# LayerNorm of the GLU's first tile placed among the last forward segments; weight turns, last turns and stores regrouped around it

## The chip, the cores and the metric

The kernel runs on one core of a Trainium2 chip. The metric is the device time of one execution in microseconds (us), taken as the median over runs. A core has a matrix engine (TensorE, "PE" in the profile, with its weight loads listed as "PEld"), a vector engine (VectorE, "DVE"), a scalar engine (ScalarE, "ACT"), a general engine (GpSimd, "POOL") and a synchronisation engine (SyncE, "SP"). Each runs its own instructions in program order; semaphores order them against each other. SP and POOL issue nearly all DMA transfers of this kernel, each on its own queue.

## The reference, cut to what matters

The computation is one block with adaptive normalisation, forward and backward. Inputs are bfloat16, x is 2048 rows of 512.

```python
mod = (silu(c) @ w_mod).reshape(1, 6, 1, -1)
sa, ca, ga, sb, cb, gb = mod[:, 0], ..., mod[:, 5]
h = layernorm(x) * (1 + ca) + sa
x = x + ga * A(h, mem0, Wq, Wk, Wv, Wo)       # attention in 64 segments
h = layernorm(x) * (1 + cb) + sb
x = x + gb * B(h, w_gate, w_up, w_down)       # GLU, F = 1792
```

A works through 64 segments of 32 rows. Each segment puts 8 memory rows ahead of its 32, projects to q, k and v (32 heads of 128), applies a masked softmax, and projects back; the first 8 rows of the result are the memory of the next segment, so the segments form a chain. B is `(sigmoid(g) * u) @ w_down` with `g = h @ w_gate` and `u = h @ w_up`. The outputs are x and the gradients of x, mem0, the seven weight matrices, c and w_mod, twelve in all, for a given `grad_out`.

## The kernel before, in words

The program has stages one after the other: the first norm and the six modulation vectors (phase 1, worked in pieces inside phase 2), the forward attention (phase 2, L437 to 962), the GLU forward and backward (phase 3, L990 on), then its weight gradients and the backward attention.

**The end of phase 2.** The loop over the 64 segments `s` (NS = 64, `s4 = s % 4`) writes, for each, in this order: k and q projections (`proj`), v projection (`v_chunk`), scores and exponentials (`st_exp`), sums of the softmax (`den`), products with v (`pv`, copies `ost`), the turned attention output (`ott`), the output projection (`outproj`, `evac_turned`), the split of its result into a high and a low bfloat16 part which TensorE adds again (`split_pair`, `sum_pair`: the tiles `at_hi`, `at_tb`, `ao_b_hi`, `ao_b_lo`), and stores for the backward pass: `OSR`, `OT` and the attention rows `AOA` in the segment, `VT` and `PS` (turned v and turned, normalised probabilities) by the function `norm` (L942), which the next segment runs. The tiles `VTr` and `Pst` are turned by a transposing DMA in all segments but the last; of segment 63 they are turned by TensorE after the loop (L951 to 961), `Pst` with the product on DVE, `VTr` with copies on ScalarE. `tail` is work put off from earlier segments (gathered rows whose projection TensorE does in chunks), and `tail.finish` ends it. `self.pin(i0)` keeps each engine's instructions in the order in which they are written.

Segment 63 also prepares phase 3. The GLU's weights and buffers lie in memory of the attention weights that have been read for the last time (`glu_tiles`, L964): w_down, the four broadcast vectors `bcs[2..5]` (ga, sb, 1 + cb, gb, each 128 x 512 in f32) and the input rings in Wv, w_gate and w_up in Wk, w_gateT and w_upT in Wq. POOL's queue loads w_gate (L834), w_up (L883) and w_down (L884); SP's queue loads the broadcasts (`mod_bc`, L369) and the rows of tile 0 and, after the loop, tile 1 (`glu_load`, L984 to 987: x, four pieces of AOA, grad_out). Both queues hold eight transfers: the profile shows an issue waiting for the transfer eight before it.

**Phase 3.** The 2048 rows form 16 tiles of 128 (NT). `run_pipeline` runs seven stages s0 to s6, one iteration after the other, in each iteration the deepest first: in iteration `it` stage `sK` works on tile `it - K`. Those that matter here:

- s0 (L1053 to 1085) is LayerNorm of a tile: DVE forms x1 = x + ga * a and its statistics, POOL the reciprocal root by a power, DVE `xhf`, the modulated rows `h2` and the gated gradient `db = gb * grad_out`; ScalarE copies `xh2`; POOL stores h2 and db (H2ROWS, DBROWS).
- s1 (L1089 and L1090) turns h2 and db into `hdT` by two transposing DMAs on SP.
- s2 (L1111 and L1115) multiplies hdT with w_gate and w_up; ScalarE applies the sigmoid (L1112).
- s3 (L1138) multiplies the turned db with w_downT; s4 (L1153) and s5 (L1178) go on with the results, with w_gateT and w_upT.

The three turned weights are made by TensorE through two buffers of PSUM (`psT`, tile `tp`), each filled by eight 128 x 128 turns at most and then copied out. w_gate's 56 turns (`wT_piece`, L1027) all stand before the pipeline, with copies on ScalarE; the dictionary `turns` (L1043) puts w_down's 56 (`wdT_piece`, L1038) at the end of iteration 2, behind s2 of tile 0, with copies alternating between DVE and ScalarE, and w_up's in iterations 3 (32) and 4 (24), alternating too.

## Time and profile before

| what | value |
|---|---|
| runs | 3063.09, 3070.22 and 3066.83 us, median 3066.83 |
| the profiled execution | 3072.34 us, its span 3070.5 us, mean granted clock 0.99 |
| busy share of TensorE, DVE, ScalarE, POOL | 97%, 52%, 42%, 40% |
| TensorE busy, 940 to 960 us | 17.90 of 20 |
| DMA share of the span's 16 engines, queue 1 and queue 0 | 62.5% and 15.5% |

The page covers one execution. Times in a list of instructions run from the span's start. A line of the timeline gives the start, the duration, the engine, the source line, the operation, output and inputs, the shape, the count, and in square brackets the time for which the engine was idle before and what released it. "tp<-ident,Wk" is a turn of w_gate or w_up, "tp<-ident,Wv" one of w_down, since the GLU's tiles are named after the memory that they lie in; for the same reason "Wq" as an output is w_gateT, w_upT or, behind the change, tile 0's rows. "PEclk" is the clock that TensorE was granted, as a share of full speed. Up to 980 us the trace shows the forward segments, from 980 on the GLU.

### The profile page before, as it was taken

What the parts mean: (1) busy time and instruction counts of PE and PEld (TensorE: products, weight loads), DVE (VectorE), ACT (ScalarE), POOL (GpSimd) and SP (SyncE); (2) the same over time, 40 slices, a digit from 0 to 9 for tenths busy, and PEclk for the clock granted to TensorE, in tenths of its full rate; (3) what the DMA queues carried; (4) which work ended last, traced back from release to release, by engine and by line L of the source; (5) the groups of instructions that cost most, each with busy time, mean ns of one, the idle gap of its engine ahead of it and who ended that gap; (6) DMA issues with size and microseconds to landing.
All of it is one profiled execution on the core that took longest, in us unless ns stands there. A gap on an engine that the chain in (4) does not pass through costs nothing.

```text
span 3070.5 us, 106490 instructions
## 1 busy us (share of the span) xinstructions
PE 2970.5 (97%) x44213; PEld 1860.3 (61%) x44289; DVE 1607.4 (52%) x3746; ACT 1286.6 (42%) x3179; POOL 1213.9 (40%) x2640
## 2 busy tenths in 40 slices
PE   5999999999997999989899999999999999999999
PEld 3666666666665444445577777777777754445454
DVE  5656656656655888732255555555555632322221
ACT  2555555555554444322255555555555520111011
POOL 2555554555554222211344444444444422333321
PEclk8999999999999999989999999999999999999999
DMA  9877877877788899987599999999999998666574
GB/s 300 217 221 204 220 216 208 220 212 209 214 219 247 200 229 232 226 264 240 169 247 245 245 251 240 249 247 247 248 242 252 244 281 268 208 193 220 185 238 148
DMA packets 839319, 703.53 MB, mean 229 GB/s; under 512 B 539730, under 2 KB 711794, under 8 KB 837940
## 3 DMA queue, kind: packets, MB, share of 16 engines
q1 hardware_dynamic: 713668, 486.69, 62.5%
q0 software_dynamic: 54512, 148.63, 15.5%
q10 hardware_dynamic: 70656, 61.41, 6.4%
q8 instruction: 348, 5.70, 0.8%
q14 instruction: 135, 1.11, 0.1%
HBM read 294.93 MB, written 276.35 MB: 186 GB/s over the span
## 4 chain that ended last, share of the span: by engine, by line
PE 47%; issue 2%; DMA 1%; POOL 0%; SPq 0%; ACT 0%; DVE 0%; POOLq 0%
PE gps L1987 11%; PE dh_ps L215 8%; PE g_ps L1649 6%; PE pass_ps L255 5%; PE gps5o L2001 4%; PE dhq_ps L223 4%; PE dh_tps L215 3%; PE dp_ps L1626 2%; PE tps L1559 2%; PE dp_ps L1634 1%; PE turn_ps L1513 1%; PE dh_ft L323 1%; POOL out_dram L1991 0%; DMA rows<-OSR 0%; DMA rows_x<-dQT 0%
## 5 line engine op out<-in xcount | busy, mean ns | idle before, releaser
L1987 PE MATMUL gps<-rows,hrows 128*128 128x512 bf16 (+2 forms) x2124 | 415.6, 355 | 1.9
L1987 PEld LDWEIGHTS <-hrows 128*128 128x128 bf16 x2160 | 211.2, 98 | 204.6
L63 DVE CAST ot<-gps 128x512 bf16<-128x512 f32 (+3 forms) x76 | 48.1, 633 | 297.1 <-PE gps L1987 200.4
L1693 POOL COPY dOst<-RAd 96x512 bf16<-96x512 bf16 x128 | 75.2, 612 | 308.9 <-DVE RAd L63 308.9
L61 ACT ACTIVATE ot<-gps 128x512 bf16<-128x512 f32 (+3 forms) x75 | 41.3, 551 | 356.4 <-PE gps L1987 241.8
L656 PE MATMUL pass_ps<-Wv,hT 128*32 128x512 bf16 (+2 forms) x2304 | 188.2, 357 | 0.0
L1991 POOL DMA_DIRECT2D out_dram<-ot x108 | 81.4, 754 | 261.4 <-DVE ot L63 135.6
L255 PEld LDWEIGHTS <-hT 128*32 128x32 bf16 x4096 | 125.0, 97 | 95.8 <-DMA Wq<-in_A_Wq_dram 6.3
L942 POOL TENSOR_TENSOR Pst<-Pst,rden 120x1408 bf16<-120x1408 bf16 x63 | 159.9, 2538 | 35.2 <-issue 22.0
L61 ACT ACTIVATE dVT<-g_ps 128x480 bf16<-128x480 f32 (+1 forms) x192 | 104.6, 545 | 96.6 <-PE g_ps L1649 96.1
L63 DVE CAST Vst<-pass_ps 96x512 bf16<-96x512 f32 x128 | 87.3, 682 | 107.5 <-ACT RBv L61 103.2
L215 PE MATMUL dh_ps<-WvT,dVT 128*32 128x512 bf16 x2048 | 134.2, 382 | 0.1
L255 PE MATMUL pass_ps<-Wq,hT 128*32 128x512 bf16 x2048 | 125.6, 383 | 6.1 <-DMA Wq<-in_A_Wq_dram 6.1
L2001 PE MATMUL gps5o<-WoT,rows 128*128 128x512 bf16 x580 | 127.8, 379 | 3.4 <-DMA rows<-OSR 2.8
L223 PE MATMUL at_ps<-Wo,OT 128*32 128x256 bf16 x4096 | 125.4, 275 | 5.2 <-DMA Wo<-in_A_Wo_dram 4.9
L656 PE MATMUL pass_ps<-Wv,hb 128*32 128x512 bf16 (+2 forms) x636 | 127.2, 345 | 0.0
L255 PE MATMUL pass_ps<-Wk,hT 128*32 128x512 bf16 x2048 | 124.1, 379 | 1.8 <-POOL hT L545 1.1
L731 POOL DMA_DIRECT2D Vst<-RBv x192 | 99.5, 523 | 62.1 <-ACT ET L778 39.2
L255 PE MATMUL pass_ps<-WoT,dyT 128*32 128x256 bf16 (+1 forms) x3072 | 122.4, 308 | 0.9 <-ACT dyT L1767 0.9
L223 PE MATMUL dhq_ps<-WqT,dQT 128*32 128x256 bf16 x4096 | 122.9, 273 | 0.0
L215 PE MATMUL dh_ps<-WkT,dKT 128*32 128x512 bf16 x2048 | 122.3, 380 | 0.0
L223 PEld LDWEIGHTS <-dQT 128*32 128x32 bf16 x4096 | 109.6, 97 | 15.9
(413 smaller groups left out, 6991.5 us busy)
## 6 DMA issues: line engine op xcount, KB each, us to landing
OSR<-Ost SPq DMA_DIRECT2D x64, 352.0 KB
OT<-OT SPq DMA_DIRECT2D x64, 352.0 KB
VT<-VTr SPq DMA_DIRECT2D x64, 352.0 KB
PS<-Pst SPq DMA_DIRECT2D x64, 352.0 KB
OT_l<-OT SPq DMA_DIRECT2D x64, 352.0 KB
Pst_l<-PS SPq DMA_DIRECT2D x64, 352.0 KB
VT_l<-VT SPq DMA_DIRECT2D x64, 352.0 KB
DVR<-rows_x POOLq DMA_DIRECT2D x64, 352.0 KB, 6.1
```

The costliest lines, as they stand in the source:

```text
L61: return nc.scalar.activation(out, in_, AF.Copy)
L63: return nc.vector.tensor_copy(out, in_)
L215: self.nc.tensor.matmul(ps[32 * j:32 * j + 32, :], lhsT=lhsT, rhs=w, start=(n < 4), stop=(n >= total - 4), tile_position=(0, 32 * j))
L223: nc.tensor.matmul(ps[32 * j:32 * j + 32, :], lhsT=x[k], rhs=w[k][:, 256 * d:256 * d + 256], start=(n == 0), stop=(n == total - 1), tile_p ...
L255: self.nc.tensor.matmul(ps[32 * j:32 * j + 32, :], lhsT=lhs(c), rhs=rhs, start=(c == 0), stop=(c == DC - 1), tile_position=(0, 32 * j))
L656: nc.tensor.matmul(ps[32 * j:32 * j + 32, o * E:(o + n) * E], lhsT=lhsT, rhs=wc[:, 3 * a + hl:3 * (a + n - 1) + hl + 1:3, :], start=(c == ...
L731: nc.gpsimd.dma_start(Vst[96 + 8 * j:104 + 8 * j, :], rb[32 * j + o:32 * j + o + 8, :])
L942: nc.gpsimd.tensor_tensor(Pst[0:120, :, :], Pst[0:120, :, :], rden[:, :].unsqueeze(2).to_broadcast([120, G, 128]), op=ALU.mult)
L1649: nc.tensor.matmul(ps[:, j, 0:w], lhsT=lh[:, g * GW:(g + 1) * GW], rhs=rh[:, g * GW:g * GW + w], start=True, stop=True)
L1987: nc.tensor.matmul(ps[:, 0:ng * E], lhsT=hrows[:, tp_, c * 128:(c + 1) * 128], rhs=rows[:, tp_, 0:ng * E], start=(tp_ == 0), stop=(tp_ == ...
L1991: nc.gpsimd.dma_start(outw[c * 128:(c + 1) * 128, h0:h0 + 3 * (ng - 1) + 1:3, :], ot[:, 0:ng * E].rearrange("p (h e) -> p h e", e=E))
L2001: nc.tensor.matmul(pss[gg][:], lhsT=src[0][:, src[1], gg * E:(gg + 1) * E], rhs=dyrows[:, tp_, :], start=(tp_ == order[0]), stop=(tp_ == o ...
```

## The change

LayerNorm of tile 0 leaves the pipeline (`s0` and `s1` return at once for j = 0) and becomes nine steps that stand in the last four segments. In segment 60 SP loads x, AOA and grad_out of tile 0, in 61 the four broadcasts, in 62 DVE forms the two gated products; in 63 follow the add (before `proj`), the statistics and the power (before `v_chunk`), the scaling, then the modulated rows and ScalarE's copy (after `outproj`), POOL's copies of the broadcasts into `bcs`, and eight turns of h2 and db on TensorE with one copy by ScalarE into `first_hdT`, in place of the two transposing DMAs. The buffers are those of phase 2 that are no longer in use, and two new small tiles in Wq's pool. A sigmoid of one column is added on ScalarE in segment 63.

The turns of segment 63 move: those of v into the segment, with copies on DVE in place of ScalarE, the store VT ahead of OSR's; those of the probabilities partly into the segment, partly ahead of `tail.finish`, with the store PS. The load of w_down moves behind `ott`; the rows of tile 1 are loaded in the segment, and what is left of tile 0's loads after it (`glu_load(0)` without x) behind PS's store.

w_gate's turns move from ahead of the pipeline into the iterations: 16 in 2 (behind w_down's), 40 in 3; w_up's are now 16 in 3 and 40 in 4. All of these are copied by ScalarE.

```diff
--- before.py
+++ after.py
...
         Wq = self.Wq = wq.tile([128, DC, H * E], BF16, name="Wq")
+        self.first_x1 = wq.tile([128, D], F32, name="x1_0")
+        self.first_st = wq.tile([128, 12], F32, name="st_0")
...
+            def first_tile_steps():
+                f32 = lambda t: t.bitcast(F32)
+                x0, ar, h2 = RB["k"][:, 0:D], RB["k"][:, D:2 * D], RB["k"][:, 0:D]
+                dout, db = RB["q"][:, 0:D], RB["q"][:, D:2 * D]
+                xhf = f32(RBv[NT % 2][:, 0:2 * D])
+                bc = {2: self.sa_bc[:], 4: self.ca1_bc[:]}
+                x1, sm = self.first_x1, self.first_st
+                def load():
+                    nc.sync.dma_start(x0, io["A_x"].rearrange("o s d -> (o s) d")[0:128, :])
+                    for i in range(4):
+                        nc.sync.dma_start(ar[32 * i:32 * i + 32, :], self.AOA[i + 1, M:M + T, :])
+                    nc.sync.dma_start(dout, io["grad_out"].rearrange("o s d -> (o s) d")[0:128, :])
+                    nc.gpsimd.memset(sm[:, 10:11], -0.5)
+                def load_mod():
+                    for i, x in ((3, "k"), (5, "q")):
+                        bc[i] = f32(btails[NT - 2][x][:].rearrange("p i x -> p (i x)"))
+                    for i in (2, 5, 4, 3):
+                        nc.sync.dma_start(bc[i], self.MODROW[:, i * D:(i + 1) * D].rearrange("o d -> (o d)").partition_broadcast(128))
+                def gates():
+                    nc.vector.tensor_tensor(db, dout, bc[5], op=ALU.mult)
+                    nc.gpsimd.dma_start(self.DBROWS[0:128, :], db)
+                    nc.vector.tensor_tensor(x1[:], ar, bc[2], op=ALU.mult)
+                def add():
+                    nc.vector.tensor_tensor(x1[:], x1[:], x0, op=ALU.add)
+                def stats():
+                    nc.vector.bn_stats(sm[:, 0:6], x1[:])
+                    nc.vector.bn_aggr(sm[:, 6:8], sm[:, 0:6])
+                    nc.vector.tensor_scalar_add(sm[:, 8:9], sm[:, 7:8], EPS)
+                    nc.gpsimd.tensor_tensor(sm[:, 9:10], sm[:, 8:9], sm[:, 10:11], op=ALU.pow)
+                def scale():
+                    nc.vector.tensor_scalar(xhf, x1[:], sm[:, 6:7], sm[:, 9:10], op0=ALU.subtract, op1=ALU.mult)
+                def rows():
+                    nc.scalar.activation(self.first_xh2, xhf, AF.Copy)
+                    nc.vector.scalar_tensor_tensor(out=xhf, in0=bc[4], scalar=1.0, in1=xhf, op0=ALU.add, op1=ALU.mult)
+                    nc.vector.tensor_tensor(h2, xhf, bc[3], op=ALU.add)
+                    nc.gpsimd.dma_start(self.H2ROWS[0:128, :], h2)
+                def mods():
+                    for i in (2, 5, 3):
+                        nc.gpsimd.tensor_copy(self.bcs[i], bc[i])
+                    nc.gpsimd.tensor_scalar_add(self.bcs[4], bc[4], 1.0)
+                def turn():
+                    tp = psp.tile([128, 2 * DC, 128], BF16, name="hd_tp", tag="p")
+                    for i in range(2 * DC):
+                        src = h2 if i < DC else db
+                        nc.tensor.transpose(tp[:, i, :], src[:, (i % DC) * 128:(i % DC) * 128 + 128], self.ident[:, :])
+                    nc.scalar.activation(self.first_hdT, tp[:], AF.Copy)
+                return load, load_mod, gates, add, stats, scale, rows, mods, turn
+            first_tile = first_tile_steps()
...
+                def turn_v(pi):
+                    ps, n = transposes_part(Vst, pi)
+                    self.evac("dve", VTr[:, pi * PG:pi * PG + n, :], ps)
+                def turn_p(pi):
+                    ps, n = transposes_part(ET, pi)
+                    nc.vector.tensor_copy(Pst[96:128, pi * PG:pi * PG + n, :], ps[96:128])
+                    nc.vector.tensor_tensor(Pst[0:120, pi * PG:pi * PG + n, :], ps[0:120],
+                                            rden[:, pi * PG:pi * PG + n].unsqueeze(2).to_broadcast([120, n, 128]), op=ALU.mult)
                 def ost(pi, or_ps, eng):
                     n = min(PG, G - pi * PG)
                     if eng == "act":
...
                 if s < NS - 1 and norms:
                     norms.pop()()
+                if s == NS - 1:
+                    first_tile[3]()
                 proj("k", 0, "dve")
                 proj("k", 1, "act")
                 if s == NS - 1:
...
                         p1(1, k)
                     v_first()
                     v_tails(0)
+                if s == NS - 1:
+                    first_tile[4]()
                 v_chunk(s, 0)
                 turns()
                 v_chunk(s, 1)
                 if s == NS - 1:
                     v_chunk(s, 2)
+                    first_tile[5]()
                 if s == 0:
                     p1(P1_AHEAD, 0)
                 if s == NS - 1:
-                    for i in (2, 4, 3, 5):
-                        self.mod_bc(None, i, "", t=self.bcs[i])
-                    self.glu_first = {0: self.glu_load(0, nc.sync)}
                     late_rows()
+                    self.glu_first = {1: self.glu_load(1, nc.sync)}
                 st_exp(0)
                 st_exp(1)
                 st_exp(2)
+                if s == NS - 1:
+                    turn_v(0)
+                    turn_v(1)
                 if s + 1 < NS:
                     v_chunk(s, 2)
                     v_tails(s + 1)
...
                     nc.sync.dma_start(Pst[:], ET[:, :], transpose=True)
                 else:
                     nc.gpsimd.dma_start(self.w_up, io["B_w_up"].rearrange("(c p) f -> p c f", p=128))
-                    nc.gpsimd.dma_start(self.w_down, io["B_w_down"].rearrange("(fc p) d -> p fc d", p=128))
                 or1 = pv(1)
                 ost(0, or0, "dve")
                 ost(1, or1, "act")
...
                 recip(2, 3, or2)
                 ost(2, or2, "dve")
                 fill(s4, "turn")
+                if s == NS - 1:
+                    turn_v(2)
                 ott(0)
                 if more:
                     mask_mm(more.pop(0))
...
                 if not early:
                     self.pop_later()
                 self.pop_later()
+                if s == NS - 1:
+                    nc.gpsimd.dma_start(self.w_down, io["B_w_down"].rearrange("(fc p) d -> p fc d", p=128))
+                    nc.sync.dma_start(self.VT[s], VTr[:])
                 nc.sync.dma_start(self.OSR[s], gl3(Ost))
                 at_ps = outproj()
                 evac_turned()
                 if s4 < 3:
                     p1(s // nseg_t + P1_AHEAD, s4 + 1)
+                if NS - 4 <= s < NS - 1:
+                    first_tile[s - NS + 4]()
+                elif s == NS - 1:
+                    first_tile[6]()
                 if s + 1 < NS:
                     tails_in("kq", s + 1)
                 parts = self.split_pair(sb2, at_ps, "at")
                 tail.collect(s4, [OT])
                 nc.sync.dma_start(self.OT[s], gl3(OT))
                 fill(s4, "f1")
+                if s == NS - 1:
+                    first_tile[7]()
+                    nc.scalar.activation(self.first_st[:, 11:12], self.first_st[:, 10:11], AF.Sigmoid)
                 if s4 == 3:
                     tail.chunk()
+                if s == NS - 1:
+                    turn_p(0)
+                    first_tile[8]()
                 ft = self.sum_pair(psp, parts, "at", "p")
                 if hT_next is not None:
                     nc.scalar.activation(hT_next[:, :, 0:M], ft[:, :, 0:M], AF.Copy)
...
                 if s < NS - 1:
                     norms.append(norm)
-            self.glu_first[1] = self.glu_load(1, nc.sync)
+            turn_p(1)
+            turn_p(2)
+            nc.sync.dma_start(self.PS[NS - 1], Pst[:])
+            self.glu_first[0] = self.glu_load(0, nc.sync)
             tail.finish()
-            for pi in range(NP):
-                ps, n = transposes_part(ET, pi)
-                nc.vector.tensor_copy(Pst[96:128, pi * PG:pi * PG + n, :], ps[96:128])
-                nc.vector.tensor_tensor(Pst[0:120, pi * PG:pi * PG + n, :], ps[0:120],
-                                        rden[:, pi * PG:pi * PG + n].unsqueeze(2).to_broadcast([120, n, 128]), op=ALU.mult)
-            nc.sync.dma_start(self.PS[NS - 1], Pst[:])
-            for pi in range(NP):
-                ps, n = transposes_part(Vst, pi)
-                self.evac("act", VTr[:, pi * PG:pi * PG + n, :], ps)
-            nc.sync.dma_start(self.VT[NS - 1], VTr[:])
-            nc.vector.tensor_scalar_add(self.bcs[4], self.bcs[4], 1.0)
             self.pinned = self.pin(i0)
     def glu_tiles(self):
...
         self.w_gateT = self.flat(Wq, 0, n).rearrange("p (c d) -> p c d", c=FC)
         self.w_upT = self.flat(Wq, n, n).rearrange("p (c d) -> p c d", c=FC)
         self.ring_dout += [self.flat(Wq, 2 * n, D)]
+        self.first_hdT = self.flat(Wq, 2 * n + D, 2 * D).rearrange("p (c x) -> p c x", x=128)
+        self.first_xh2 = self.flat(Wq, 2 * n + 3 * D, D)
     def glu_load(self, j, q):
-        q.dma_start(x0, io["A_x"].rearrange("o s d -> (o s) d")[r0:r1, :])
+        if j > 0:
+            q.dma_start(x0, io["A_x"].rearrange("o s d -> (o s) d")[r0:r1, :])
         for i in range(4):
             q.dma_start(a_rows[32 * i:32 * i + 32, :], self.AOA[4 * j + i + 1, self.cfg.M:self.cfg.M + self.cfg.T, :])
         q.dma_start(dout, io["grad_out"].rearrange("o s d -> (o s) d")[r0:r1, :])
...
-            turns = {2: [wdT_piece(c) for c in range(DC)],
-                     3: [wT_piece(w_up, w_upT, 0, 8, 0)], 4: [wT_piece(w_up, w_upT, 8, 6, 0)]}
+            turns = {2: [wdT_piece(c) for c in range(DC)] + [wT_piece(w_gate, w_gateT, 0, 4, None)],
+                     3: [wT_piece(w_gate, w_gateT, 4, 10, None), wT_piece(w_up, w_upT, 0, 4, None)],
+                     4: [wT_piece(w_up, w_upT, 4, 10, None)]}
...
                 load(j + 1)
                 st = ins.pop(j)
+                if j == 0:
+                    st.update(x1=self.first_x1, rstd=self.first_st[:, 9:10], xh2=self.first_xh2)
+                    return st
                 a_rows = st["a_rows"]
...
                 return st
             def s1(j, st):
+                if j == 0:
+                    st["hdT"] = self.first_hdT
+                    return st
                 hdT = sbp.tile([128, 2 * DC, 128], BF16, name="hdT", bufs=2)
                 nc.sync.dma_start(hdT[:, 0:DC, :], st["h2"][:], transpose=True)
                 nc.sync.dma_start(hdT[:, DC:2 * DC, :], st["db"][:], transpose=True)
...
             ET = mybir.EngineType
-            wT_piece(w_gate, w_gateT, 0, FC, None)()
             later = after
             def after(it):
```

## The prediction

> **What bounds the kernel now.** I read the page first: TensorE is busy for 2970.5 of 3070.5 us, 97%, and the costliest lines of the chain of waits are all TensorE's, so time is won only where TensorE stands still. The 40 slices show one dip at slice 13. The table of stages, cut into 20 us pieces, puts it between the last forward segment and the GLU (columns: stretch, length, busy us of PE, PEld, DVE, ACT, POOL, then granted clock, DMA share, GB/s).
>
> ```profile
> 960.00:980.00 20.00, 17.53 (x314) 11.46 (x307) 9.94 (x27) 8.48 (x23) 8.38 (x11) 0.97 0.98 354
> 980.00:1000.00 20.00, 5.36 (x60) 4.34 (x59) 12.10 (x24) 9.98 (x13) 5.03 (x11) 0.67 0.70 218
> ...
> 1020.00:1040.00 20.00, 17.76 (x128) 10.16 (x128) 16.80 (x28) 9.90 (x16) 5.52 (x10) 1.00 1.00 238
> 1040.00:1060.00 20.00, 19.95 (x104) 9.57 (x104) 16.28 (x31) 7.48 (x13) 3.81 (x7) 1.00 0.90 211
> ```
>
> From 1040 on TensorE is full, so whatever the stretch 960 to 1044 gains stays gained to the end. The timeline there, in order of time, names the waits:
>
> ```profile
> 976.17 0.69 DVE L313 TENSOR_TENSOR ao_b_lo<-ao_tps,ao_b_hi 128x512 bf16<-128x512 f32 x1 [0.87 <-ACT ao_b_hi L312]
> ...
> 978.59 0.43 DVE L953 COPY Pst<-tps 32x512 bf16<-32x512 bf16 x1
> 979.05 0.69 DVE L954 TENSOR_TENSOR Pst<-tps,rden 120x512 bf16<-120x512 bf16 x1
> ...
> 980.09 1.91 PE L1027 MATMUL tp<-ident,Wk 128*128 128x128 bf16 x16
> ...
> 983.84 1.47 POOL L709 DMA_DIRECT2D AOA<-ao_b_rb  x3 [3.01 <-DMA Wv<-in_B_w_down_dram]
> ...
> 985.61 0.69 DVE L1059 TENSOR_TENSOR t<-Wv 128x512 f32<-128x512 bf16 x1 [3.36 <-DMA Wv<-AOA]
> ...
> 997.23 1.20 SPq L1089 DMA_TRANSPOSE hdT<-h  x1
> ...
> 999.68 1.67 PE L1111 MATMUL mm<-Wk,hdT 128*128 128x448 bf16 x4 [13.15 <-DMA hdT<-h]
> ...
> 1007.14 0.94 PE L1038 MATMUL tp<-ident,Wv 128*128 128x128 bf16 x14
> ...
> 1007.73 0.62 DVE L63 COPY w_downT<-tp 128x896 bf16<-128x896 bf16 x1 [2.04 <-PE tp L1038]
> ...
> 1014.30 0.92 PE L1111 MATMUL mm<-Wk,hdT 128*128 128x448 bf16 x4
> ...
> 1022.06 1.00 ACT L61 ACTIVATE Wq<-tp 128x1024 bf16<-128x1024 bf16 x1
> ...
> 1029.17 0.92 PE L1111 MATMUL mm<-Wk,hdT 128*128 128x448 bf16 x4
> ...
> 1044.26 3.19 PE L1153 MATMUL mm<-Wv,hhT 128*128 128x512 bf16 x14
> ```
>
> TensorE turns w_gate (980.09 to 986.5) and then stands for 13.15 us until the transposed rows of tile 0 arrive; stage s2 of tile 0 starts at 999.68. That is the prize. The reader should also see two smaller things: POOL waited 3.01 us for w_down to land, at 983.84, and DVE had all of LayerNorm of tiles 0, 1 and 2 behind it before the first w_downT copy at 1007.73.
>
> **The change, part by part.** Times below are the profiled execution's (span 3070.5 us, 3072.34 us in all; the median of the runs shown, 3066.83, is 5.5 lower). Its marks are carried forward from the order in which the built instructions stand on each engine.
>
> *Early loads and the first norm (segments 60 to 63).* SP gets six more issues (x rows, four of AOA, grad_out; some 0.45 us each by L984, L986, L987) ahead of OT's store in segment 60, and the four broadcasts (2.03 us by L369) in 61. OT's next write is 10 us after its store, so 3 us are covered; without that slack ScalarE and DVE would wait for the store up to that length. The broadcasts leave the stretch 965 to 983, where SP's next issues waited 3.4, 3.3, 2.2 and 2.0 us for them. DVE's seven added operations fall into its idle times: two products (0.69 each) into 2.13 us before at_lo, the add into 0.76, statistics (0.69, 0.18, 0.15) into 1.03, the scaling (0.55) and two VTr copies (0.43 each) into 1.83. POOL's power (0.57) makes w_up's issue 0.7 late, the DBROWS issue (0.54) delays only tail copies that nothing needs for 7 us. Cost nothing, up to 0.5 us if a cover fails.
>
> *The tail of segment 63.* The third VTr copy (0.36) stands before OT's copy: the output projection slips 0.36. ScalarE gets the xh2 copy (0.63) in an idle 1.19, then table load 1.28, a Sigmoid of one column (0.20, as L156's) and the hdT copy (1.02 by the 128x1024 copies) before ao_b_hi: at_hi ends 972.30, table and Sigmoid 973.8, hdT 974.87, ao_b_hi 975.5 instead of 974.24. DVE then does ao_b_lo, at_tb and the turns of P 1 and 2 (2.06 us, 979.77 to 981.83 before) ahead of the last ao_b_lo, which slips from 976.17 to 978.6 (the first Pst copy, at 973.4, needs segment 62's PS store, which SP's wait shows landed at 970.3). The chain behind it is 1.94 us to TensorE's end (978.11) and 2.37 to DVE's: TensorE is free for the GLU at about 980.6, DVE at 981.0.
>
> The page "ScalarE: Activation LUTs" (Trainium skill, section "What ACT_TABLE_LOAD costs") adds a drain of 1.38 us to the 1.28 of a table load; the trace's load at 47.61 is followed by its ACTIVATE at 48.90, with no drain. By the page DVE would be free 1.4 later, at 982.4, and POOL's wait, below, would still end later: the sum would be the same.
>
> *POOL.* The four copies of the broadcasts to Wv have no row (f32 to f32): between four of the 0.76 cast and four of the 1.55 product, 3.0 to 6.2 us from 973.4; I take 3.0 (the cast is the nearer form). Both ends lie before its next work at 980.2, so either costs nothing. w_down's issue (1.10) moves from 965.38 to 970.8. POOL then issues nine AOA stores (0.5 each); the seventh needs w_down landed, as it did before (the 3.01 us), and behind them stands the power of tile 1. When does w_down land? Before, it took 18.4 us from issue to 983.84 among as many bytes: 1.0 MB of broadcasts and 0.4 of tile 0 go from this stretch, 1.1 MB of VT, OSR and OT stores and most of a PS store come in. It queues behind w_up either way, so I take 984.5; ends 982 (w_up out of the way sooner) and 989.2 (18.4 us from the new issue). Two more stores, a memset and the semaphore put the power's start 1.7 later, 986.2, and xhf of tile 1 at 986.85; without w_down it would be 985.65.
>
> *DVE in the GLU.* s0 of tile 0 is gone, but s0 of tiles 1 and 2 now start at 981 instead of 994 and 999.86, and all of it stands before the first w_downT copy. From xhf of tile 1 to the end of tile 2's db the rows show 997.34 to 1005.69, 8.35 us: the first w_downT copy starts at 995.2 (before 1007.73), 10.7 after w_down. s2 of tile 0 runs at 980.6; TensorE was nearly idle from 977, so I charge the half clock (0.50 in the stretch after the old wait) for its first 3.7 us: end 988.5. It turns 14 blocks of w_down and then waits for DVE and ScalarE, some 5 us: s2's early start is not the path, DVE is. So the new waits of s2's first Sigmoid and u for the stores of VT and OSR, whose memory they reuse, have 5 us of cover.
>
> *To s2 of tile 1.* Before, 6.57 us from that copy to 1014.30. Added: 16 turns of w_gate (0.9) and a new half-clock start, some 0.2: 995.2 + 7.7 = 1002.9. Gain 11.4 here.
>
> *The turns of w_gate and w_up, now 56 and 40 in iterations 3 and 4 (32 and 24 before), all copied by ScalarE.* In 3, s2 of tile 1 ends at 1008.95, but ScalarE first has xh2 of tile 3, whose xhf DVE ends 9.2 after the last w_downT copy (1000.0, as before): the last u ends at 1011.0. Seven copies at 1.02 and 0.01 between follow; TensorE's last turns need the fifth (1016.15), then come four matmuls of s4 and, at 1017.5, s3 (3.02): s2 of tile 2 at 1020.5 against 1029.17. The gain falls to 8.7. In 4, xhf of tile 4 ends 10.6 after s3's start (1026.15 to 1036.79 before), at 1028.1; xh2 and u, then five copies, the fifth to 1034.5; two matmuls and 14 of dgT: s4 of tile 1 at 1038.0 against 1044.26. Before, DVE took half of these copies, 0.64 each.
>
> **Sum: 6.3 us.** In parts: s2's start 19.1 earlier; less 6.6 for the wait behind DVE's two norms (12.5 left), 1.1 for the new turns and clock (11.4), 2.7 for seven copies in iteration 3 (8.7), 2.4 for five in 4 (6.3). Profiled execution 3072.3 to 3066.0; median 3066.8 to 3060.5.
>
> TensorE then has one new wait of 2.35 us in iteration 4 (1028.1 to 1030.45). Rows bound its clock: a wait of 1.48 at 1037.4 left it at 1.00, the thin stretch from 975.5 brought it to 0.50 for 3.3 us. I take no drop, the nearer row, and keep 1.6 us for the range. The page "TensorE: Matmul & The Clock Gate" (Trainium skill, section "What's actually happening") lowers the clock after an idle window of about 3.4 us, which gives none here and a drop in the 5 us wait ahead of w_downT; the sum by it is the same 6.3.
>
> **Rivals.** (1) *The copies and POOL cost less*: w_down is early (gain 1.2), the 128x1024 copies run at the 0.93 mean of 981.19 to 987.7 (12 times 0.09, 1.1), and the P turns don't delay the tail (2.0): 4.3 more, 3056.2. For it: that mean; against: the copies in the GLU took 1.00 to 1.02. (2) *w_down as late as its new issue*: 989.2, every microsecond costs one: 6.3 less 4.7, 3065.2. For it: the POOL wait; against: w_up was in front in both. (3) *Slower: SP's queue*. Behind PS's store (978.8) stand ten issues up to tile 2's AOA rows, each waiting for the one eight before it to land. At the 0.55 of 985 to 997 with PS's wait they land at 987.5, and DVE needs them at 989.35. At the 2.5 of 970 to 983 (970.29, 973.88, 977.65, 980.04, 982.59) they land at 1006: 16.6 late, 3077. It breaks even at 995.6, 1.5 us an issue. Against: w_gate and w_up are then gone. (4) *The change wins all its 19 us*: not possible while the w_downT copies stand behind two norms on DVE; under 2%.
>
> **Chances and range.** About 0.2%, 6.1 us, is what a measurement of this kernel tells from none. Main case 0.50, half of it beyond 6.1; rival 1 0.22, rival 2 0.18, rival 3 0.10. So faster 0.47, same 0.43, slower 0.10. The range runs from rival 1 less 1.7 us of the runs' own spread (3054.5) to a break-even plus 2 (3069); rival 3 beyond that is left out.
>
> **What would show it.** Right: the first s2 matmul at 979 to 983 with no wait on hdT; the first w_downT copy of DVE at 994 to 998, at the end of an unbroken s0 of tile 2, with a TensorE wait of 4 to 6 us before it; a POOL wait on w_down before the last AOA stores; seven Wq copies in a row on ScalarE and TensorE waiting for them. Wrong: w_downT copied before 992, or a DVE wait on AOA rows ahead of tile 2's t, or a lower clock after 1025.

## The result, and the profile after

The changed kernel takes 3061.01 us in the median of 22 runs (3055.93 to 3064.80), the kernel before 3066.36 in as many. The ratio is 0.9979 with a 95% interval of 0.9973 to 0.9985, a gain of 0.21% where 0.2% was forecast (3060.5 us).

Single executions of one kernel spread by 9 to 11 us, more than the gain, so the traces are compared from a common point: the first k projection of segment 58, at 887.24 us of the span before and 883.76 after. (The texts of e9 and e11 call it that of segment 60. Counted back from segment 63, the last one, segment 60's own comes 28.86 us later in both traces; the change begins behind that.) The last point taken is the first modulation sum of s6 (the matmuls into `acc_ps`, 1056.45 before and 1047.40 after), from where TensorE is full. From there to the end the fourteen profiles of this study take 2006.9 to 2015.6 us. Before and e2, which run the same code there, take 2014.1 and 2007.3, so I read that part as jitter. Between the two points lie 169.21 us before and 163.64 after: the change is worth 5.57 us in its own stretch.

The stages of the changed kernel (columns as in the table before):

```profile
960.00:980.00 20.00, 17.11 (x280) 10.81 (x278) 12.99 (x34) 9.65 (x23) 10.61 (x18) 1.00 1.02 381
980.00:1000.00 20.00, 13.40 (x110) 8.03 (x109) 16.04 (x28) 10.35 (x16) 5.40 (x11) 0.91 0.65 194
1000.00:1020.00 20.00, 18.02 (x124) 10.64 (x123) 11.64 (x19) 12.52 (x18) 3.75 (x7) 0.91 0.94 202
1020.00:1040.00 20.00, 17.94 (x117) 9.55 (x116) 12.55 (x24) 10.78 (x16) 3.38 (x7) 1.00 0.63 158
1040.00:1060.00 20.00, 20.00 (x106) 9.68 (x105) 17.65 (x33) 7.47 (x13) 5.45 (x10) 1.00 0.91 219
```

TensorE is busy for 13.40 of the 20 us from 980 on, where it had 5.36, but it is not full again before 1040: three stretches hold 10.6 us of gaps together. Its timeline names most of them:

```profile
976.89 0.92 PE L1205 MATMUL mm<-Wk,Wq 128*128 128x448 bf16 x4
...
985.05 1.55 PE L1209 MATMUL mm<-Wk,Wq 128*128 128x448 bf16 x4 [4.21 <-ACT sg L1206]
986.39 1.70 PE L1205 MATMUL mm<-Wk,Wq 128*128 128x448 bf16 x4
...
991.67 0.55 PE L1125 MATMUL tp<-ident,Wv 128*128 128x128 bf16 x7 [1.73 <-ACT w_downT L61]
...
999.23 0.92 PE L1205 MATMUL mm<-Wk,hdT 128*128 128x448 bf16 x4
...
1008.30 0.82 PE L1247 MATMUL mm<-Wv,hhT 128*128 128x512 bf16 x3 [1.96 <-DMA hhT<-hh]
...
1018.43 0.92 PE L1205 MATMUL mm<-Wk,hdT 128*128 128x448 bf16 x4
...
1028.10 0.61 PE L1114 MATMUL tp<-ident,Wk 128*128 128x128 bf16 x8 [1.92 <-ACT Wq L61]
```

The 13.15 us for hdT are gone: s2 of tile 0 starts as soon as the tail of the segments ends. In their place stand 4.21 us in the middle of s2, 1.73 for the copies of w_downT, 1.96 for the transposed hh and 1.92 for the copies of w_upT. On DVE, ScalarE and POOL:

```profile
980.04 0.69 DVE L1150 TENSOR_TENSOR t<-Wv 128x512 f32<-128x512 bf16 x1 [2.72 <-DMA Wv<-AOA]
...
986.37 0.69 DVE L1150 TENSOR_TENSOR t<-Wv 128x512 f32<-128x512 bf16 x1 [0.42 <-DMA Wv<-AOA]
...
991.52 0.68 DVE L1173 TENSOR_TENSOR db<-Wk,Wv 128x512 bf16<-128x512 bf16 x1
992.12 1.15 DVE L63 COPY w_downT<-tp 128x896 bf16<-128x896 bf16 x2
```

```profile
968.69 1.28 ACT L1008 ACT_TABLE_LOAD   x1
969.98 0.20 ACT L1008 ACTIVATE st<-st 128x1 f32<-128x1 f32 x1
...
983.93 0.63 ACT L1166 ACTIVATE xh<-xhf 128x512 bf16<-128x512 f32 x1 [9.70 <-DVE xhf L1165]
984.47 0.53 ACT L1206 ACTIVATE sg<-mm 128x448 bf16<-128x448 f32 x1
...
1027.03 4.67 ACT L61 ACTIVATE Wq<-tp 128x1024 bf16<-128x1024 bf16 x5
```

```profile
979.86 0.99 POOL L771 DMA_DIRECT2D AOA<-ao_b_rb  x2 [0.27 <-DMA Wv<-in_B_w_down_dram]
...
982.05 0.50 POOL L771 DMA_DIRECT2D AOA<-ao_b_rb  x1 [1.20 <-DMA AOA<-at_rb]
...
982.74 0.58 POOL L1161 TENSOR_TENSOR rstd<-ve,mhalf 128x1 f32<-128x1 f32 x1
```

DVE's first copy of w_downT follows the last product of tile 2's norm with no gap, and ScalarE's first sigmoid follows the copy xh2 of tile 1, for which it had stood 9.70 us.

### The profile page after: what moved, and what is told of

It is laid out like the page before. It is cut to its first block, busy times and chain, and to the rows that moved or that the text cites. A ratio compares the mean times of both kernels' runs of the same rounds, so it can differ in the third digit from the quotient of the medians.

```text
span 3063.0 us, 106593 instructions
## 1 busy us (share of the span) xinstructions
PE 2975.5 (97%) x44297; PEld 1859.8 (61%) x44297; DVE 1605.9 (52%) x3744; ACT 1288.2 (42%) x3182; POOL 1220.6 (40%) x2645
```

## The experiments

Each kernel was timed beside the kernel before, and its ratio is to that: the median of before was 3065.05 us beside e1 to e4, 3065.74 beside e5 to e8 and 3065.36 beside e9 to e12. "Marks" are us after the first k projection of segment 58, of one profiled execution each: the last matmul of the tail (a turn into `ao_b_tp`, called the fold), the start of s2 of tile 0, the first w_downT copy on DVE, the start of s2 of tiles 1 and 2, and the first modulation sum.

| kernel | median, us (runs) | ratio to before, 95% | fold | s2 (0) | w_downT | s2 (1) | s2 (2) | sum |
|---|---|---|---|---|---|---|---|---|
| before | 3066.36 (22) | | 90.80 | 112.44 | 120.49 | 127.06 | 141.93 | 169.21 |
| changed | 3061.01 (22) | 0.9979 [0.9973, 0.9985] | 93.06 | 93.13 | 108.36 | 115.47 | 134.67 | 163.64 |
| e1 turns in front | 3057.45 (5) | 0.9968 [0.9956, 0.9981] | 93.07 | 99.72 | 108.53 | 115.86 | 130.58 | 157.87 |
| e2 turns moved only | 3069.34 (11) | 1.0012 [1.0003, 1.0021] | 90.82 | 112.99 | 121.82 | 129.41 | 146.09 | 175.07 |
| e3 norm only | 3057.42 (11) | 0.9975 [0.9966, 0.9984] | 91.28 | 99.99 | 107.72 | 114.07 | 134.08 | 161.36 |
| e4 changed, second norm later | 3058.01 (7) | 0.9975 [0.9964, 0.9986] | 98.95 | 99.01 | 108.78 | 116.29 | 135.23 | 162.72 |
| e5 as e3, second norm later | 3054.67 (12) | 0.9974 [0.9966, 0.9983] | 93.28 | 101.03 | 107.67 | 114.16 | 137.31 | 165.53 |
| e6 as e1, second norm later | 3054.91 (9) | 0.9974 [0.9964, 0.9984] | 93.05 | 99.41 | 106.05 | 112.54 | 128.92 | 157.46 |
| e7 alternating copies | 3058.90 (11) | 0.9979 [0.9970, 0.9988] | 97.56 | 97.63 | 112.04 | 119.14 | 135.82 | 164.19 |
| e8 xh2 later | 3059.96 (11) | 0.9986 [0.9977, 0.9995] | 96.92 | 96.99 | 110.83 | 119.37 | 135.94 | 164.92 |
| e9 own buffer | 3060.16 (11) | 0.9981 [0.9973, 0.9990] | 93.06 | 93.14 | 109.09 | 117.57 | 134.04 | 163.02 |
| e10 as e1, own buffer | 3056.11 (8) | 0.9972 [0.9961, 0.9982] | 93.06 | 99.54 | 108.63 | 114.72 | 133.38 | 160.66 |
| e11 as e6, own buffer | 3052.76 (5) | 0.9961 [0.9948, 0.9973] | 93.06 | 99.48 | 106.13 | 112.62 | 129.28 | 157.51 |
| e12 no early sigmoid | 3058.69 (11) | 0.9980 [0.9972, 0.9989] | 93.06 | 93.12 | 109.49 | 116.99 | 136.02 | 164.99 |

The theory is that of the prediction: the wait for hdT goes, DVE's two norms ahead of the w_downT copies give a third of it back, the moved turns another third. The rivals are that the turns' place is harmless, that s2 of tile 0 is on the path, or that the moved stores carry the gain. A mark comes from a single profile, and kernels with the same code differ by up to 3.9 us between two marks (below), so a step counts as shown only where several rows agree.

**e1, w_gate's turns back in front.**

```diff
-            turns = {2: [wdT_piece(c) for c in range(DC)] + [wT_piece(w_gate, w_gateT, 0, 4, None)],
-                     3: [wT_piece(w_gate, w_gateT, 4, 10, None), wT_piece(w_up, w_upT, 0, 4, None)],
-                     4: [wT_piece(w_up, w_upT, 4, 10, None)]}
+            turns = {2: [wdT_piece(c) for c in range(DC)],
+                     3: [wT_piece(w_up, w_upT, 0, 8, 0)], 4: [wT_piece(w_up, w_upT, 8, 6, 0)]}
...
+            wT_piece(w_gate, w_gateT, 0, FC, None)()
```

> The changed kernel with w_gate's 56 turns back in one piece ahead of the pipeline and w_up's back at 32 and 24 with alternating copies: the early norm and the moved turns and stores stay. My theory: the turns of w_gate cost nothing there, because ScalarE, which copies them, would only wait for xhf of tile 1 (9.70 us in the changed kernel's profile) and the first w_downT copy on DVE stays where it is (992.1); iterations 2 to 4 then lose the copies that I charged with 1.1, 2.7 and 2.4 us, less the 2.0 that hhT's transposing DMA takes there in any case: 3 to 5 us faster than the changed kernel, 3056 to 3058 us. Rival: ahead of the pipeline they push s2 of tile 0 back by seven copies, 6.5 us, and the w_downT turns with it: no faster than the changed kernel, 3061 to 3065.

3057.45 us, as the theory had it. s2 of tile 0 starts 6.6 us later than in the changed kernel and the first w_downT copy 0.17: the 56 turns are free in front, since DVE isn't there earlier. The modulation sum comes 5.8 us sooner. The runs alone don't tell e1 from the changed kernel (the intervals overlap), but two later pairs that differ in the turns' place point the same way. Against the kernel before, turns in front are 2.3 us faster in e1 than in the changed kernel, 3.8 in e6 than in e4 and 4.1 in e10 than in e9; by the marks 5.8, 5.3 and 2.4.

**e2, only the turns moved**, in the kernel before (the edit of e1 the other way round).

> The kernel before with only w_gate's turns moved into iterations 2 and 3 and w_up's to 3 and 4, all copied by ScalarE; no early norm, no moved store. My theory: the 13.15 us wait ahead of s2 of tile 0 stays and grows by the turns that filled it, since nothing that hdT needs comes earlier, and iterations 2 to 4 get the added copies: 4 to 6 us slower than before, 3070.5 to 3072.5. Rival: the place of the turns is without effect, TensorE has as many of them in all: 3066.

Slower than before: 3069.34 against 3065.05, ratio 1.0012, and 5.86 us at the modulation sum: 0.55 at s2 of tile 0, then 1.80 to s2 of tile 1, 1.81 to that of tile 2 and 1.70 to the sum. The median lies just below the 3070.5 to 3072.5 that was expected, the 4.3 us above before within the 4 to 6. TensorE's wait is longer, for the same transfer:

```profile
998.48 1.68 PE L1112 MATMUL mm<-Wk,hdT 128*128 128x448 bf16 x4 [20.07 <-DMA hdT<-h]
```

So this part of the change takes 2 to 6 us, with the early norm and without it.

**e3, only the early norm.**

```diff
+                    nc.gpsimd.dma_start(self.w_down, io["B_w_down"].rearrange("(fc p) d -> p fc d", p=128))
...
-                if s == NS - 1:
-                    turn_v(0)
-                    turn_v(1)
...
-                    turn_p(0)
...
-            turn_p(1)
-            turn_p(2)
-            nc.sync.dma_start(self.PS[NS - 1], Pst[:])
             self.glu_first[0] = self.glu_load(0, nc.sync)
             tail.finish()
+            for pi in range(NP):
+                turn_p(pi)
+            nc.sync.dma_start(self.PS[NS - 1], Pst[:])
+            for pi in range(NP):
+                ps, n = transposes_part(Vst, pi)
+                self.evac("act", VTr[:, pi * PG:pi * PG + n, :], ps)
+            nc.sync.dma_start(self.VT[NS - 1], VTr[:])
```

With it goes the edit of e1.

> The kernel before with only the early LayerNorm of tile 0: w_gate's turns ahead of the pipeline, the last turns of v and of the probabilities after the tail with VT's and PS's stores behind them, w_down issued right behind w_up, all as before. My theory: the early norm carries most of the gain; the late stores take 1 to 3 us of it, since buffers of the GLU reuse the memory of VTr and Pst and wait for them (2.59 us on db before): 3057 to 3061 us. Rival 1: the moved turns and stores are worth nothing, the same as with them (3056 to 3058). Rival 2: they carry the gain, and the norm alone is within 2 us of before: 3065 or more.

3057.42: the early norm alone gains as much as the whole change (at the modulation sum 2.3 us more), and the moved turns and stores on top of it (e1) show no gain that these runs can tell (0.9975 against 0.9968, the intervals overlap). The fold comes 1.8 us earlier without P's turns ahead of it, the price that rival 1 of the prediction had set at 2.0. In its profile TensorE waits 4.4 us for hhT, where e1's waited 0.3.

**e4, the second norm later.** Tile 2's s0 goes behind s2 of tile 1.

```diff
             def s0(j):
+                if j == 2:
+                    return {}
+                return norm_rows(j)
...
             def s1(j, st):
+                if j == 2:
+                    st.update(norm_rows(2))
```

> The changed kernel with s0 of tile 2 taken out from ahead of the w_downT copies and put behind s2 of tile 1 in iteration 3, on all engines. My theory: DVE's two norms ahead of the w_downT copies set s2 of tile 1; with one of them gone the first w_downT copy comes as soon as TensorE has turned 14 blocks (989.9 against 992.1), s2 of tile 1 starts 2 us earlier; but ScalarE then has two xh2 copies ahead of w_gate's turns, the second behind 12 us of norms on DVE, and s2 of tile 2 wins nothing: 3059 to 3062 us. Rival: DVE isn't what the w_downT turns wait for, and s2 of tile 1 starts no earlier than 15.47 us behind the last w_downT-free mark, s2 of tile 0 plus 22.3 us, as in the changed kernel: 3061 or more.

Faster than expected by 1 us (3058.01), which the intervals don't tell from the changed kernel. DVE has the one norm done before TensorE has turned its blocks, and now waits for TensorE:

```profile
991.27 0.69 DVE L1178 TENSOR_TENSOR db<-Wv 128x512 bf16<-128x512 bf16 x1
993.91 0.62 DVE L63 COPY w_downT<-tp 128x896 bf16<-128x896 bf16 x1 [1.95 <-PE tp L1125]
```

TensorE itself is late in this profile, so it doesn't settle alone what set this step. e6 does, where the tail ends in time: DVE's wait is longer, and its first copy comes 2.5 us earlier than in e1, so that the order on DVE had set the step.

```profile
991.67 0.62 DVE L63 COPY w_downT<-tp 128x896 bf16<-128x896 bf16 x1 [3.84 <-PE tp L1125]
```

The same profile of e4 shows what nobody had priced. DVE's early copy of v into VTr stands 4.78 us, with TensorE behind it, and then TensorE runs at half its clock (the output projection takes 3.24 us, 1.93 in the changed kernel):

```profile
969.16 0.76 DVE L63 COPY VTr<-tps 128x512 bf16<-128x512 bf16 x2 [4.78 <-issue]
```

```profile
970.08 0.22 PE L844 MATMUL or_ps<-ones,ET 128*128 128x1 bf16 x3 [3.96 <-DVE rden L849]
...
972.19 3.24 PE L223 MATMUL at_ps<-Wo,OT 128*32 128x256 bf16 x64
```

The fold came 5.9 us late. DVE's row doesn't name what it waits for, but the one earlier reader of VTr is segment 62's store of VT, and SP's queue shows when that landed: the issue eight behind it waits for it.

```profile
SPq L1073 <- DMA VT<-VTr: 2.6, 1, 2.6
```

```profile
969.10 0.30 SPq L1073 DMA_DIRECT2D Wv<-AOA  x1
```

The store, issued at 959.26 among the loads of the weights (DMA share about 1), landed at 969.10, and DVE's copy follows at 969.16. Three of the seven profiles with the early turns into VTr show this wait (e4, e7, e8), and in all three DVE starts 0.06 us behind that issue of SP. In the other four (changed, e1, e6, e12) SP's issue has no such wait, and DVE has none for the store.

**e5 and e6, the second norm later** in e3 and in e1 (the edit of e4).

> The kernel before with the early LayerNorm of tile 0 alone (as in the run with the norm only), and s0 of tile 2 put behind s2 of tile 1 in iteration 3. My theory: two waits are left in the run with the norm only, DVE's second norm ahead of the w_downT copies and the 4.4 us for hhT, whose transposing DMA SP issues behind the rows of later tiles and the two transposes of tile 2. With the second norm later both shrink, since hdT of tile 2 goes behind hhT: s2 of tile 1 some 1.5 us earlier, the wait for hhT under 1 us, 3 to 5 us faster than with the norm only, 3052 to 3055 us. Rival: hhT's transfer itself is what takes the time (7 to 9 us from its issue), and the wait for it stays: 3056 to 3058.

> The changed kernel with w_gate's turns ahead of the pipeline and s0 of tile 2 behind s2 of tile 1. My theory: as with the norm only, 2 to 4 us faster than with the turns in front alone (3057.45 measured), so 3053 to 3055.5 us. Rival: TensorE has no time left in that stretch, since w_gate's turns end at 986 and s2 of tile 0 at 992, where DVE is free in any case; then it is 3056 to 3058. In some executions the early copies of v into VTr will wait for segment 62's store of VT (4.78 us in the profile of the run with the second norm later), which this kernel has and the one with the norm only has not.

Both medians lie where they were expected, 3054.67 and 3054.91, but the ratios, 0.9974 each, don't set them apart from e1 and e3. e5's profile shows another thing than was expected: the wait for hhT is gone, and a wait of TensorE of 6.89 us for hdT of tile 2 has come, since SP now has its transposes behind those of duT and dgT (the last of them took 7.22 us of SP's queue). In e6 s2 of tile 1 comes 3.3 us sooner than in e1 and the modulation sum 0.4: TensorE then waits 1.62 us for a copy of w_upT that DVE makes behind two norms.

**e7, alternating copies.**

```diff
-            turns = {2: [wdT_piece(c) for c in range(DC)] + [wT_piece(w_gate, w_gateT, 0, 4, None)],
-                     3: [wT_piece(w_gate, w_gateT, 4, 10, None), wT_piece(w_up, w_upT, 0, 4, None)],
-                     4: [wT_piece(w_up, w_upT, 4, 10, None)]}
+            turns = {2: [wdT_piece(c) for c in range(DC)] + [wT_piece(w_gate, w_gateT, 0, 4, 0)],
+                     3: [wT_piece(w_gate, w_gateT, 4, 10, 0), wT_piece(w_up, w_upT, 0, 4, 0)],
+                     4: [wT_piece(w_up, w_upT, 4, 10, 0)]}
```

> The changed kernel with the copies of w_gate's and w_up's turns shared by DVE and ScalarE in turn, as w_up's were before, in place of ScalarE alone; the turns stay in the iterations 2 to 4. It tells the place of the turns from the choice of the engine that copies them. My theory: the place is what costs, 12 more copies in iterations that are bound by their copies and by hhT; sharing them wins 1 to 2 us at most, since DVE comes to its share only behind the norm of tile 3 (1007) and of tile 4: 3059 to 3061 us. Rival: ScalarE alone is the loss; shared, the change is as fast as with the turns in front: 3056 to 3057.5.

3058.90, just below what was expected, ratio as the changed kernel's. The rival, 3056 to 3057.5, is not borne out. Whether sharing wins the 1 to 2 us isn't told (this profile has the wait on VTr, too); from s2 of tile 1 to the modulation sum it took 45.05 us, and three kernels with the same code there and ScalarE alone (changed, e9, e12) took 48.17, 45.45 and 48.00.

**e8, xh2 later.**

```diff
-                nc.scalar.activation(xh2[:], xhf[:], AF.Copy)
+                if j < 4:
+                    xh_late.append((xh2, xhf))
+                else:
+                    nc.scalar.activation(xh2[:], xhf[:], AF.Copy)
...
                 for f in turns.pop(it, []):
                     f()
+                if it > 1:
+                    xh_copies()
```

`xh_copies` makes the copies that `xh_late` holds.

> The changed kernel with ScalarE's copies xh2 of tiles 1 to 3 put behind the turns of the iteration after, so that s2's sigmoids no longer stand behind xhf. In the changed kernel's profile s2 of tile 0 stands 4.21 us in its middle for that reason. My theory: DVE's two norms set the w_downT copies, so the earlier end of s2 of tile 0 (983 in place of 989.2) only makes a wait of 7 us there; s2 of tile 1 at most 0.5 us earlier by it; the w_gate copies in iteration 3 start 1.5 us sooner but wait for hhT: 0 to 1.5 us in all, 3059.5 to 3061. Rival: s2 of tile 0 is on the path, and 4 us are won: 3057.

3059.96, no gain. s2 of tile 0 now runs without a gap (the wait on VTr made it start 3.9 us late here), and the time goes into the wait behind it, as the waits of TensorE show (us in total, times, longest):

```profile
PE tp L1125 <- DVE w_downT L63: 6.0, 1, 6.0
PE tp L1114 <- ACT Wq L61: 2.7, 2, 1.9
PE or_ps L844 <- DVE rden L849: 2.1, 1, 2.1
```

**e9 to e11, an own buffer for v of segment 63.**

```diff
+                VTl = Vsts[(s + 1) % 2][:, :].rearrange("p (g x) -> p g x", g=G)
...
-                    self.evac("dve", VTr[:, pi * PG:pi * PG + n, :], ps)
+                    self.evac("dve", VTl[:, pi * PG:pi * PG + n, :], ps)
...
-                    nc.sync.dma_start(self.VT[s], VTr[:])
+                    nc.sync.dma_start(self.VT[s], VTl)
```

> The changed kernel, but the turned v of segment 63 goes into the Vst buffer that segment 62 has left, not into VTr, so that its copies on DVE no longer wait for segment 62's store of VT. Three profiles of kernels with the early turns of v show that wait (4.78, 3.87 and 2.94 us on DVE, TensorE idle for 4.0, 3.1 and 2.1 and the last fold of the tail 98.95, 97.56 and 96.92 us after the first k projection of segment 60), three, that of the changed kernel among them, do not (93.06). My theory: the early turns of v made a new wait for a store that the weights' loads hold up, which comes in about half of the executions; without it the last fold lies at 93.1 in the profile, and the median falls by 1 to 2.5 us against the changed kernel: 3058.5 to 3060. Rival: the stretch was slow for another reason (the clock, DMA share), and the median stays at 3061.

> The changed kernel with w_gate's turns ahead of the pipeline and v of segment 63 in its own buffer. If both losses are as read from the profiles and independent, 3053 to 3056 us (3057.45 with the turns in front alone, less 1 to 2.5). Rival: the gain of the own buffer is taken by the next wait (rows of tile 1, w_down): 3056 to 3058.

> As the run before this one, and s0 of tile 2 behind s2 of tile 1. In the profile with the turns in front this was worth 0.4 us at the first modulation sum (157.87 to 157.46 after the first k projection of segment 60): it wins 3.3 us at s2 of tile 1 and gives them back where w_upT's last copies on DVE come late (a wait of 1.62 us before s5). So 0 to 1 us faster than without it: 3052.5 to 3056. Rival: the hdT of tile 2, now late, makes s2 of tile 2 wait as in the run with the norm only (6.9 us): 3057 or more.

No profile of the three has the wait, and the fold lies at 93.06 in all. But e9's 3060.16 is within the noise of the changed kernel's 3061.01, so the 1 to 2.5 us that I expected are not shown; how often the wait comes stays open. In the marks little of the wait is left at the end: the fold comes 3.9 to 5.9 us late in e4, e7 and e8, yet their modulation sums (162.7 to 164.9) lie where those of changed, e9 and e12 do (163.0 to 165.0). e10 lies between theory and rival (3056.11). e11, with w_gate's turns in front, the second norm later and the own buffer, has the lowest median of all: 3052.76 in 5 runs, ratio 0.9961, 12.6 us below before. Its interval touches the changed kernel's and overlaps those of e1, e3 to e6 and e10. DVE there waits 3.71 us for TensorE's turns of w_down, so that TensorE sets the pace from s2 of tile 0 to the w_downT copies:

```profile
979.99 0.69 DVE L1156 TENSOR_TENSOR t<-Wv 128x512 f32<-128x512 bf16 x1 [2.95 <-DMA Wv<-AOA]
...
989.61 0.62 DVE L63 COPY w_downT<-tp 128x896 bf16<-128x896 bf16 x1 [3.71 <-PE tp L1127]
```

**e12, no early sigmoid.**

```diff
-                    nc.scalar.activation(self.first_st[:, 11:12], self.first_st[:, 10:11], AF.Sigmoid)
```

> The changed kernel without the sigmoid of one column in segment 63, so that ScalarE loads its table (1.28 us) ahead of s2's first sigmoid. My theory: no difference, 3060 to 3062 us: s2 of tile 0 ends 1.3 us later (990.4), TensorE's 14 turns of w_down at 991.3, and DVE comes to their copies at 992.1 in any case. Rival: the load lies on the path from xhf of tile 1 to w_downT and costs 1.3 us, 3062.3, or 2.7 with a drain ahead of it, 3063.7.

3058.69, ratio 0.9980 against 0.9979: no difference, as expected (the median lies 1.3 us below the range given). The table load stands ahead of s2's first sigmoid, TensorE waits 5.02 us there, and DVE still makes its first w_downT copy right behind tile 2's norm (994.63 after 994.03).

## Why the prediction was right, point by point

Marks in the prediction's time, that of the profile before; those of the changed kernel's profile carry 3.48 us more.

| step | predicted | measured |
|---|---|---|
| TensorE free, s2 of tile 0 starts | 980.6 | 980.37 |
| ScalarE's early table load and sigmoid end | 973.8 | 973.66 |
| DVE free of the tail | 981.0 | 980.79 |
| POOL's power for tile 1 starts | 986.2 | 986.22 |
| xhf of tile 1 | 986.85 | 986.83 |
| first w_downT copy on DVE | 995.2 | 995.60 |
| s2 of tile 1 | 1002.9 | 1002.71 |
| s2 of tile 2 | 1020.5 | 1021.91 |
| s4 of tile 1 | 1038.0 | 1038.69 |

- **The signs that were named.** Of those for "right" the first s2 matmul, the first w_downT copy and POOL's wait on w_down (0.27 us) came. The unbroken norm of tile 2, the wait of 4 to 6 us ahead of the w_downT copies and the seven Wq copies in a row did not. One sign for "wrong" came: DVE waited 0.42 us for AOA rows ahead of tile 2's t. So the sum held better than the path that it was built on.
- **The prize and its cap.** s2's start won 19.3 us and only 11.6 of it reached s2 of tile 1, because all of tile 2's norm stands on DVE ahead of the w_downT copies. e8 shows that s2 of tile 0 isn't the path (TensorE waits 6.0 us for DVE behind it), e6 and e11 that the second norm is. Rival 4 (all 19 us) is out.
- **The waits of tile 1's norm.** The times hold, the names only half. DVE was to begin at once and POOL to wait for w_down. In the profile DVE first waits 2.72 us for tile 1's rows; POOL gets past w_down at 983.34 (predicted 984.5), waits 1.20 for one of its own stores, and is free within 0.2 us of DVE's `ve`. Two chains ended together, and the prediction had one of them; that its errors cancel to 0.02 us is luck. In e3, w_down is issued at its old place, 5.3 us earlier by the marks (78.17 against 83.45), and POOL gets past it at 95.98 against 96.10: the later issue made it no later, and rival 2 is out.
- **s2 of tile 0.** I had it run through, at half clock for its first 3.7 us, with a wait of 5 us behind it. It ran at full clock for five groups (in e9, with the same code there, the half clock came at its start, 0.50 from 978 to 981) and then stood 4.21 us, since I had left out that xh2 of tile 1 lies ahead of its sigmoids on ScalarE, and only then at half clock. The cost is nothing, for the reason above (e8).
- **The copies of the turns.** 1.1, 2.7 and 2.4 us were charged, 6.2 in all. By the marks e2 measures 5.9 and e1 5.8, and by the medians it is 2.3 to 4.3, so the sum was right or 2 to 4 us too high. The parts were not as predicted. In iteration 3 TensorE waited not for ScalarE but for hhT, and then ran at half clock; s2 of tile 2 came 19.2 us after that of tile 1 (17.6 predicted), and 16.47 in e9, whose profile has neither. This is the step that was mis-sized in the changed kernel's profile, by 1.6 us. In iteration 4 the copies were the wait, and five of them took 4.67 us, 0.93 each in a row, where I had taken 1.02; TensorE waited 1.92, predicted 2.35.
- **SP's queue.** Rival 3 did not come as it was written: SP reaches PS's store at 982.08, 3.3 us later than predicted, but issues the ten behind it at 0.57 us each (979.13 to 984.86), so tile 2's rows cost DVE 0.42 us. A small one of its kind did. hh is ready at 997.14, and SP turns to it at 1001.01, behind rows of later tiles and the transposes of tile 2, and hhT lands at 1008.3:

```profile
997.71 0.43 SPq L1074 DMA_DIRECT2D Wq<-in_grad_out_dram  x1
998.24 1.30 SPq L1183 DMA_TRANSPOSE hdT<-h  x1
999.64 1.21 SPq L1184 DMA_TRANSPOSE hdT<-db  x1
1001.01 2.43 SPq L1225 DMA_TRANSPOSE hhT<-hh  x1
```

- **Nothing for the tail's added work.** In the changed kernel's profile that holds: at_hi comes 0.21 us late, predicted 0.36. The covers named were OT's store and SP's issues; the one that fails in e4, e7 and e8, by 2.9 to 4.8 us on DVE, is the store of VT, which the prediction did not list among those that the moved copies wait for.
- **The clock.** No drop was taken for iteration 4, and its wait of 1.92 us brought none. In iteration 3, where no wait was foreseen, the 1.96 us for hhT brought one. In the changed kernel's 2 us stretches (columns as before):

```profile
1008.00:1010.00 2.00, 1.70 (x12) 1.19 (x13) 1.36 (x2) 0.64 (x2) 0.65 (x2) 0.77 1.15 255
1010.00:1012.00 2.00, 2.00 (x12) 1.29 (x11) 0.00 (x0) 1.32 (x2) 0.00 (x0) 0.50 1.30 83
...
1028.00:1030.00 2.00, 1.90 (x22) 1.35 (x22) 1.97 (x3) 2.00 (x4) 1.44 (x3) 1.00 0.37 131
```

The sum was 6.3 us; 5.57 were measured between the marks and 5.35 between the medians. Some of the closeness is luck: kernels with the same code from s2 of tile 1 to the sum differ there by up to 3.9 us (e1 took 42.01, e10 45.94, with waits for hhT of 0.3 and 2.9). Two terms may have erred together as well: e1 and e10, the change with the turns in front, gain 11.3 and 8.6 us by the marks and 7.6 and 9.3 by the medians, where the prediction had 12.5 left ahead of the turns. What the prediction did not ask is whether the change's parts belong together. The early norm alone gains as much as the whole or more, and the moving of w_gate's turns takes 2 to 6 us back: they had filled TensorE's time while DVE made the norms, and that time stayed.

## What to carry to other kernels

Where a wait is removed, look what else had been placed into it: work that filled a wait is free only there, and taking it out together with the wait charges it in full later. Follow the next wait on each engine in program order, the cheap copies too, and check each moved write against the last transfer that reads its buffer. Judge by marks inside the trace when single runs spread by more than the effect, but by several profiles, since one may miss a wait that another has. Where an engine's row doesn't name its wait, look on the DMA queue for the issue that waits for the same transfer.

## What the runs showed of the hardware

- **Half clock after short waits.** TensorE fell to 0.50 after waits of 3.96, 3.06, 2.13 and 1.96 us (e4, e7, e8, changed), for 3.3 to 3.5 us and in e4 for 6.8, and the output projection took 3.21 to 3.50 us in place of 1.93 in the first three. In e5 it fell without any wait over 0.42 us there, after four microseconds in which TensorE was busy for 3.00; in e3 the same stretch with 2.97 of 4 busy kept its clock. e5, in stretches of 2 us:

```profile
963.47:965.47 2.00, 1.58 (x30) 1.09 (x24) 1.50 (x4) 1.25 (x5) 2.00 (x3) 1.00 0.99 377
965.47:967.47 2.00, 1.42 (x28) 1.14 (x26) 1.26 (x4) 1.50 (x6) 0.41 (x1) 1.00 1.00 385
967.47:969.47 2.00, 1.97 (x33) 1.28 (x34) 0.82 (x3) 1.63 (x5) 0.57 (x1) 0.65 1.04 429
```

  The Trainium skill ("TensorE: Matmul & The Clock Gate", section "What's actually happening") tells of a free-running window and of an idle one of about 3.4 us that lowers the clock. That the same stretch falls in one run and not in another agrees with a free-running window; the drops after 2.13 us and after 0.42 show that such a window need not be idle from end to end.
- **A transposing DMA under load.** hhT (128 x 1792) landed 7.3 us after SP's issue in the changed kernel and 9.0 in e3 (1002.14 to 1011.10), and the store of VT took 9.8 us from its issue in e4 (959.26 to 969.10), while the weights were loading.
- **A table load without a drain.** The sigmoid starts 0.01 us after the load of 1.28 (968.69 to 969.98), the same in e12.
- **POOL's copies, f32 to f32.** The 128 x 512 copies, which had no row before, took 0.61 us each, less than the 0.76 that bounded them from below, and the one that adds 1 took 1.51; the four took 3.22 from the first one's start to the last one's end (970.07 to 973.29), where 3.0 was taken.
